# A fused attention and feed-forward kernel: the weight join, the casts and the order of the opening are changed

## The chip, the cores and the metric

The kernel runs on one NeuronCore of one Trainium2 chip. The metric is the device time of one execution in microseconds (us). The core has five engines that run side by side, each in the order of its own instruction queue: TensorE (PE in the profile, with PEld for its weight loads), VectorE (DVE), ScalarE (ACT), GpSimd (POOL) and SyncE (SP), which here only issues DMA transfers.

## The reference

Block-window attention with summaries, then a feed-forward layer with a piecewise gate. Only what matters:

```python
batch, n_heads, seq, head_dim = (4, 8, 768, 64)       # q, k, v, fp32
block, window = (32, 16)
k_sum = k.reshape(B, H, nb, block, D).max(axis=3)     # 24 summary keys per sequence
v_sum = v.reshape(B, H, nb, block, D).mean(axis=3)    # 24 summary values
scores = concat(window scores with |i - j| < 16, scores on k_sum + log(32))
x = softmax(scores) @ concat(v, v_sum)                # heads side by side: 3072 tokens x 512
h = x @ w_in                                          # 512 -> 2048
g = where(h >= 1, h, where(h <= -1, 0, (h + 1)**2 / 4))
out = g @ w_out                                       # 2048 -> 512
```

The weights w_in and w_out come as 64-bit floating-point numbers, which the engines don't compute with. So the kernel turns each into a 32-bit number from its two 32-bit words: sign, exponent and upper mantissa bits from the top word, the last three bits from the low word.

## The kernel before, in words

The 3072 tokens are worked through in eight chunks of 384 tokens (T), two for each sequence. A chunk's attention is done for four pairs of heads; its feed-forward (FF) layer runs over sixteen slices f of 128 hidden units. Products of the FF layer keep fp32 accuracy by splitting both operands into a high part (cast to fp32r) and the rest: three products for one.

The order is written out by hand. `OPENING`, `SECOND` and `LATER` are lists of steps; a step is a letter, which names a function in the table `steps`, and hexadecimal digits, its arguments. Each engine gets its instructions in the order of the list. `OPENING` covers all of chunk 0, the conversion of all weights and chunk 1's attention. `SECOND` and `LATER` run the FF layer of a chunk with the attention of the next between it; a step that was done already is skipped there.

The attention steps, by chunk, pair of heads and often head: `r`, `y` load the raw keys and values of a sequence for the summaries, `k`, `v`, `q` the windows and queries, `m` the mask and an identity matrix. `K` lays out chunk 0's key windows, `R` takes the summary keys (maximum), `C` copies them behind the windows, `Y`, `Z`, `V`, `W` do the same for the values: sum on VectorE, transpose on TensorE, mean on ScalarE (L267), spread over the six blocks on GpSimd (L271). `S` is the score product, `M` adds the mask and takes the maxima, `E` the exponentials, `D` the reciprocals (an add, L306, and a reciprocal, L307), `N` the norm on GpSimd (L311), `T` a transpose on TensorE, `P` its copy out, `A` the value product, `X` and `L` the high part and the rest of x.

The weight steps, for each of sixteen pairs of weight pieces (512 columns each): `w` fetches, `a` (L139) and `b` (L144) scale the top and the low word on ScalarE, `c` joins the words on VectorE, `d` casts to the high part (`convert_high`, on GpSimd for even pairs and ScalarE for odd ones), `e` subtracts it on GpSimd (L172). Pair i holds w_out's slice i-1 and w_in's slice i+1.

The FF steps: `F` (L421, four parts per slice) is the first product, `G`, `H`, `I`, `J` the gate and its high part, `O` (L450, GpSimd) the rest, `B` (L459) the second product. `U` and `o` take out and store the result.

`j` (L429) writes filler products on TensorE: fp32 products of a 128 x 128 tile of zeros with itself whose result nobody reads. The last digit of the step is their number.

Buffers limit how early a step can run: the tiles of kind "k", "q" and "v" have two buffers each; the converted words and the raw keys and values share three (`stage`, tag "w"); PSUM gives six banks to the joins and the attention of the opening, three of which hold the result of chunk 0 from its first `B` on.

Of the kernel before, what the change touches and what calls it, by code (L numbers as in the profile page):

```python
# [45 lines left out]
H01 G02 I01 H02 F030 F031 F032 I02 F033 F040 F041 w6 w7 w8 a6 w9 F042 F043 J01 b6 b7 c5 O01 G03 H03 I03 B01 d4 e4
F050 F051 d5 F052 F053 J02 J03 O02 B02 O03 B03 v10 v11 a7 a8 a9 e5 G04 G05 H04 H05 b8 c6 c7 d6 d7 e6 e7 I05 F060 F061
F062 F063 q10 q11 I04 F070 F071 F072 F073 J04 O04 J05 O05 B04 B05 b9 c8 c9 d8 e8 wa aa ba wb ab bb G06 H06 I06 J06
F080 F081 F082 F083 O06 B06 ca d9 e9 da ea G07 H07 I07 F090 F091 G08 H08 I08 F0a0 F0a1 F0a2 F0a3 F092 F093 J07 J08
# [533 lines left out]
```

## Time and profile before

| | us |
|---|---|
| median of 3 runs | 657.27 |
| lowest and highest | 656.46, 657.53 |
| profiled execution, its time | 656.5 |
| profiled execution, its span | 654.5 |
| TensorE busy | 630.8 (96%) |
| VectorE busy | 372.3 (57%) |
| ScalarE busy | 345.1 (53%) |
| GpSimd busy | 259.4 (40%) |

The span is the time from the first to the last instruction in the trace; the 2.0 us between it and the execution's time lie around it. Busy time of TensorE counts the filler products too. A row of a profile names the source line (L421), the engine, the operation, what is written and read, the number of instructions, and in brackets what ended the idle time in front of them.

### The profile page before, as it was taken

What the parts mean: (1) busy time and instruction counts of PE and PEld (TensorE: products, weight loads), DVE (VectorE), ACT (ScalarE), POOL (GpSimd) and SP (SyncE); (2) the same over time, 40 slices, a digit from 0 to 9 for tenths busy, and PEclk for the clock granted to TensorE, in tenths of its full rate; (3) what the DMA queues carried; (4) which work ended last, traced back from release to release, by engine and by line L of the source; (5) the groups of instructions that cost most, each with busy time, mean ns of one, the idle gap of its engine ahead of it and who ended that gap; (6) DMA issues with size and microseconds to landing.
All of it is one profiled execution on the core that took longest, in us unless ns stands there. A gap on an engine that the chain in (4) does not pass through costs nothing.

```text
span 654.5 us, 11884 instructions
## 1 busy us (share of the span) xinstructions
PE 630.8 (96%) x4442; PEld 561.3 (86%) x4442; DVE 372.3 (57%) x837; ACT 345.1 (53%) x881; POOL 259.4 (40%) x272
## 2 busy tenths in 40 slices
PE   7789999679999999999999999999999999999997
PEld 7688997568898989889898988889898888999996
DVE  5899983638773735838571746838671744511111
ACT  3789974735454645454454645444364636433332
POOL 1659985524342333333333333324333332322221
PEclk9989999889999999999999999999999999999999
DMA  8999700474121325034301324034211410000001
GB/s 283 326 343 296 268 2 22 134 227 142 40 69 38 117 61 143 28 89 135 88 21 37 119 61 143 18 89 144 74 35 37 118 37 2 2 21 29 1 1 48
DMA packets 49769, 63.57 MB, mean 97 GB/s; under 512 B 24880, under 2 KB 33328, under 8 KB 49712
## 3 DMA queue, kind: packets, MB, share of 16 engines
q1 hardware_dynamic: 49712, 62.81, 31.4%
q8 instruction: 35, 0.57, 0.4%
q14 instruction: 22, 0.18, 0.1%
HBM read 56.51 MB, written 6.29 MB: 96 GB/s over the span
## 4 chain that ended last, share of the span: by engine, by line
PE 85%; DVE 4%; DMA 4%; POOL 2%; ACT 2%; issue 2%; SPq 1%; POOLq 0%; ACTq 0%; DVEq 0%
PE acc L459 39%; PE h L421 37%; PE o_ps L410 3%; DMA first<-in_kT 3%; PE s_ps L355 2%; PE o_ps L327 1%; DMA vraw<-in_vT 1%; PE t_ps L316 1%; POOL glo L450 1%; DVE turned_blocks L400 1%; ACT e L301 1%; POOL halves L172 1%; PE h_idle L429 1%; DVE w L159 0%; PE s_ps L283 0%
## 5 line engine op out<-in xcount | busy, mean ns | idle before, releaser
L421 PE MATMUL h<-xhi,halves 128*128 128x384 f32 x1024 | 283.9, 339 | 2.2 <-DVE t L440 1.6
L459 PE MATMUL acc<-halves,ghi 128*128 128x512 f32 x768 | 240.7, 394 | 0.0
L450 POOL TENSOR_TENSOR glo<-t,ghi 128x384 fp32r<-128x384 f32 x128 | 130.0, 1017 | 267.4 <-ACT ghi L445 173.8
L421 PEld LDWEIGHTS h<-xhi,halves 128*128 128x128 f32 x1024 | 188.0, 188 | 9.0 <-issue 2.2
L440 DVE SCALAR_TENSOR_TENSOR t<-h,t 128x384 f32<-128x384 f32 x128 | 71.2, 557 | 215.1 <-ACT t L437 204.7
L421 PE MATMUL h<-xlo,halves 128*128 128x384 f32 x512 | 173.5, 339 | 0.0
L459 PEld LDWEIGHTS acc<-halves,ghi 128*128 128x128 f32 x768 | 144.8, 188 | 28.7
L459 PE MATMUL acc<-halves,glo 128*128 128x512 f32 x384 | 154.6, 402 | 0.4 <-POOL glo L450 0.4
L434 ACT ACTIVATE t<-h,ones_half 128x384 f32<-128x384 f32 x128 | 74.2, 580 | 123.2 <-PE h L421 119.8
L445 ACT CAST ghi<-t 128x384 fp32r<-128x384 f32 x128 | 65.4, 513 | 119.8 <-DVE t L440 119.4
L400 DVE STREAM_TRANSPOSE turned_blocks<-e 32x192 f32<-32x192 f32 x288 | 106.5, 370 | 22.0 <-POOL e L388 17.9
L421 PEld LDWEIGHTS h<-xlo,halves 128*128 128x128 f32 x512 | 96.5, 188 | 5.4
L459 PEld LDWEIGHTS acc<-halves,glo 128*128 128x128 f32 x384 | 72.1, 188 | 15.1 <-issue 1.9
L437 ACT ACTIVATE t<-t 128x384 f32<-128x384 f32 x128 | 66.9, 523 | 3.2
L376 ACT ACTIVATE e<-e,den 128x120 f32<-128x120 f32 x144 | 55.3, 387 | 24.2 <-DVE den L370 24.2
L388 POOL TENSOR_TENSOR e<-e,den 128x720 f32<-128x720 f32 x24 | 33.4, 1391 | 48.7 <-DVE den L382 25.5
L172 POOL TENSOR_TENSOR halves<-w,halves 128x1024 fp32r<-128x1024 f32 x16 | 38.6, 2416 | 3.3 <-ACT halves L166 2.7
L376 ACT ACTIVATION_READ_ACCUMULATOR e<-e,den 128x1 f32 x144 | 27.5, 191 | 0.0
L429 PE MATMUL h_idle<-zeros 128*128 128x128 f32 x162 | 23.4, 304 | 1.0 <-POOL zeros L112 1.0
L301 ACT ACTIVATE e<-e,den 128x120 f32<-128x120 f32 x48 | 18.3, 384 | 10.7 <-DVE den L296 10.6
L429 PEld LDWEIGHTS h_idle<-zeros 128*128 128x128 f32 x162 | 21.8, 216 | 1.6 <-POOL zeros L112 1.0
L363 DVE SCALAR_TENSOR_TENSOR e<-s_ps,mask_sb 128x360 f32<-128x360 f32 x48 | 22.2, 524 | 0.0
(78 smaller groups left out, 455.0 us busy)
## 6 DMA issues: line engine op xcount, KB each, us to landing
k<-in_kwin SPq DMA_DIRECT2D x28, 360.0 KB, 4.1
v<-in_vwin SPq DMA_DIRECT2D x30, 288.0 KB, 3.3
raw<-in_w_in SPq DMA_DIRECT2D x16, 512.0 KB, 10.4
raw<-in_w_out SPq DMA_DIRECT2D x16, 512.0 KB, 10.6
out<-o SPq DMA_DIRECT2D x24, 256.0 KB, 2.3
q<-in_q SPq DMA_DIRECT2D x56, 96.0 KB, 4.2
kraw<-in_kT SPq DMA_DIRECT2D x13, 384.0 KB, 4.6
vraw<-in_vT SPq DMA_DIRECT2D x13, 384.0 KB, 5.8
```

The source lines that it names most:

```text
L172: nc.gpsimd.tensor_tensor(out=lo, in0=converting[i].bitcast(F32), in1=hi.bitcast(F32), op=ALU.subtract)
L376: nc.scalar.activation(out=e, in_=e, func=AF.Exp, bias=dens[c, p][:, 0, j, t:t + 1], scale=1.0, accum_out=dens[c, p][:, 1, j, t:t + 1])
L388: nc.gpsimd.tensor_tensor(out=e, in0=e, in1=den.unsqueeze(2).broadcast_to([P, 2 * NT, KA]), op=ALU.mult)
L400: nc.vector.transpose(out=pt[kb * SB:(kb + 1) * SB, :, qb * SB:(qb + 1) * SB], in_=e[qb * SB:(qb + 1) * SB, :, at:at + SB])
L421: nc.tensor.matmul(hs[c, f][:, :T], weight["win", f][w][:, k * P:(k + 1) * P], x, start=(k == 0 and n == 0), stop=(k == NK - 1 and n == 2))
L429: nc.tensor.matmul(hs["idle"][:, :P], zeros, zeros, start=True, stop=True)
L434: nc.scalar.activation(out=ts[c, f], in_=hs[c, f][:, :T], func=AF.Relu, bias=ones_half, scale=0.5)
L437: nc.scalar.square(out=ts[c, f], in_=ts[c, f])
L440: nc.vector.scalar_tensor_tensor(out=ts[c, f], in0=hs[c, f][:, :T], scalar=1.0, in1=ts[c, f], op0=ALU.max, op1=ALU.min)
L445: nc.scalar.copy(out=hi, in_=ts[c, f])
L450: nc.gpsimd.tensor_tensor(out=lo, in0=ts[c, f], in1=hi.bitcast(F32), op=ALU.subtract)
L459: nc.tensor.matmul(acc[c][i], a[:, rows], weight["wout", f][w], start=(f == 0 and n == 0), stop=(f == NF - 1 and n == 2))
```

## The change

- The join (`c`) is done in two instructions for each half of a pair instead of three. The first shifts the top word left by three and ORs the low word into it; the second ORs the sign bit in. The integer add is gone. Since the low word is now ORed, `b` scales it so that it never exceeds seven. The four instructions of a pair are four steps of their own in the list (`c10` to `c13`).
- All casts to the high part (`d`) run on GpSimd. The subtractions (`e`) of pairs 1, 5, 9 and 13 run on VectorE, the others stay on GpSimd.
- The value means are kept in a tile of their own for each pair of heads, so that chunk 1, of the same sequence, only spreads them again (`W`): its steps `Z` and `V` are gone, and `W` writes six blocks where it wrote five.
- `M` is cut into a mask step `M` and a maximum step `f` for each head, `m` into mask and identity.
- `OPENING` has a new order. Chunk 1's attention stands between the FF steps of chunk 0, further first products of chunk 1 and loads for chunk 2 stand in it, and its `j` steps are others.

```diff
@@ the order of the opening, up to chunk 0's first FF product and a little beyond
 OPENING = """
-m r00 K00 R00 C00 q00 r01 R01 q01 K01 C01 y01 j00f S00 j013 S01 M00 M01 E000 D000 E001 D001 y00 E010 N000 j02e T000
-P000 E011 r02 K02 R02 C02 q02 Y01 N001 j038 T001 w0 a0 D010 N010 Y00 j041 Z00 Z01 r03 K03 v00 v01 V00 W00 D011 N011
-R03 C03 P001 y02 S02 M02 b0 c0 d0 e0 E020 V01 W01 j054 A00 T010 P010 T011 P011 q03 j063 S03 M03 X00 L00 E021 D021
-N021 D020 N020 Y02 j07f j085 Z02 w1 a1 E030 D030 N030 y03 E031 D031 N031 Y03 j096 Z03 b1 c1 w2 b2 a2 v02 V02 W02 A01
-X01 T021 P021 T020 P020 L01 c2 w3 b3 a3 v03 V03 W03 j0a4 A02 T031 P031 T030 P030 j0b3 A03 X02 L02 d1 d2 X03 L03 w4 a4
-b4 c3 F000 F001 F002 F003 G00 H00 I00 F010 F011 F012 F013 e1 F020 c4 F021 F022 F023 e2 w5 a5 b5 J00 O00 B00 d3 e3 G01
...
+q00 r00 r02 R00 K00 C00 r01 m0 q02 j00f j01f j02f j03f S00 R02 M000 K01 f000 R01 q01 K02 w0 M001 r03 C01 E000 D000 C02
+j04f j059 S01 M010 f010 E010 y02 f001 y01 N000 y00 M011 f011 m1 j065 S02 E001 b0 D001 a0 N001 v00 j07f j08f j099 T000
+K03 R03 T001 P001 P000 Y00 Z00 w1 c01 M020 C03 c00 V00 W00 M021 E011 q03 v01 y03 D010 f021 N010 D011 E021 Y01 f020
+j0af j0b2 A00 c03 c02 N011 j0cf j0d2 S03 Y02 b1 T010 T011 E020 M030 M031 d0 X00 Z01 V01 D021 a1 Z02 W01 P010 V02 P011
+w2 j0ef j0f2 A01 N021 f030 E030 D020 Y03 T021 L00 N020 T020 f031 X01 E031 v02 e0 D030 L01 v03 F000 Z03 c10 F010 W02
+P021 c12 c11 P020 b2 a2 N030 F001 c13 V03 A02 D031 X02 T030 c20 P030 c21 N031 L02 T031 w4 k10 q10 F011 w3 q11 P031 W03
+d1 k11 A03 X03 c23 F002 a4 w6 c22 d2 L03 F003 e1 F012 F013 G00 H00 G01 C10 H01 I00 I01 S10 M101 e2 f101 w7 b4 c40 J00
+c41 J01 F020 c42 F021 F022 F030 O01 F031 b3 w5 F032 F023 O00 c43 d4 F033 M100 a3 C11 k12 G02 B00 f100 c31 q12 c30 c32
...
-HI_POOL = [0, 2, 4, 6, 8, 10, 12, 14]
+REST_VECTOR = [1, 5, 9, 13]
...
-        nc.scalar.mul(out=low, in_=low.bitcast(U32), mul=2.0 ** -29)
-
-    def convert_join(i):
+        nc.scalar.mul(out=low, in_=low.bitcast(U32), mul=7.49 * 2.0 ** -32)
+
+    def convert_join(i, n):
 
         low, top = raws[i]
-        w = converting[i] = stage.tile([P, 2 * DM], I32, tag="w", name=f"w{i}", bufs=W_BUFS)
-        c_ps = [ps.tile([P, DM], I32, tag="ps", name=f"c{i}_{part}") for part in range(2)]
-        cols = [slice(part * DM, (part + 1) * DM) for part in range(2)]
-        for part in range(2):
-            nc.vector.tensor_scalar(out=c_ps[part], in0=top[:, cols[part]], scalar1=3, scalar2=0x7FFFFFF8,
-                                    op0=ALU.logical_shift_left, op1=ALU.bitwise_and)
-        for part in range(2):
-            nc.vector.scalar_tensor_tensor(out=c_ps[part], in0=top[:, cols[part]], scalar=-0x80000000, in1=c_ps[part],
+        what, part = divmod(n, 2)
+        cols = slice(part * DM, (part + 1) * DM)
+        if what == 0:
+            joined[i, part] = ps.tile([P, DM], I32, tag="ps", name=f"c{i}_{part}")
+            nc.vector.scalar_tensor_tensor(out=joined[i, part], in0=top[:, cols], scalar=3, in1=low[:, cols],
+                                           op0=ALU.logical_shift_left, op1=ALU.bitwise_or)
+        else:
+            if i not in converting:
+                converting[i] = stage.tile([P, 2 * DM], I32, tag="w", name=f"w{i}", bufs=W_BUFS)
+            nc.vector.scalar_tensor_tensor(out=converting[i][:, cols], in0=top[:, cols], scalar=-0x80000000, in1=joined[i, part],
                                            op0=ALU.bitwise_and, op1=ALU.bitwise_or)
-        for part in range(2):
-            nc.vector.tensor_tensor(out=w[:, cols[part]], in0=c_ps[part], in1=low[:, cols[part]], op=ALU.add)
 
     def convert_high(i):
         halves[i] = room(i, "halves", [P, 2, 2 * DM], F32R)
-        if i in HI_POOL:
-            nc.gpsimd.tensor_copy(out=halves[i][:, 0], in_=converting[i].bitcast(F32))
-        else:
-            nc.scalar.copy(out=halves[i][:, 0], in_=converting[i].bitcast(F32))
+        nc.gpsimd.tensor_copy(out=halves[i][:, 0], in_=converting[i].bitcast(F32))
...
     def convert_rest(i):
         hi, lo = halves[i][:, 0], halves[i][:, 1]
-        nc.gpsimd.tensor_tensor(out=lo, in0=converting[i].bitcast(F32), in1=hi.bitcast(F32), op=ALU.subtract)
+        eng = nc.vector if i in REST_VECTOR else nc.gpsimd
+        eng.tensor_tensor(out=lo, in0=converting[i].bitcast(F32), in1=hi.bitcast(F32), op=ALU.subtract)
...
-        nc.scalar.mul(out=v_ts[c, p][KW:KA, 0], in_=vs_pss[c, p][:NSUM, :P], mul=1.0 / SB)
+        v_mean[p] = att.tile([P, P], F32, tag=f"mean{p}", name=f"mean{c}_{p}", bufs=1)
+        nc.scalar.mul(out=v_mean[p][KW:KA], in_=vs_pss[c, p][:NSUM, :P], mul=1.0 / SB)
 
     def spread_vals(c, p):
-        mean = v_ts[c, p][KW:KA]
-        nc.gpsimd.tensor_copy(out=mean[:, 1:], in_=mean[:, :1].broadcast_to([NSUM, NB - 1, P]))
+        nc.gpsimd.tensor_copy(out=v_ts[c, p][KW:KA], in_=v_mean[p][KW:KA].unsqueeze(1).broadcast_to([NSUM, NB, P]))
...
-    def masks(c, p):
+    def masks(c, p, j):
...
+    def maxima_of_head(c, p, j):
...
-        if "idle" not in hs:
-            hs["idle"] = ps_h.tile([P, 512], F32, tag="h", name="h_idle")
+        if ("idle", stage_) not in hs:
+            hs["idle", stage_] = ps_h.tile([P, 512], F32, tag="h", name=f"h_idle{stage_}")
         for _ in range(n):
-            nc.tensor.matmul(hs["idle"][:, :P], zeros, zeros, start=True, stop=True)
+            nc.tensor.matmul(hs["idle", stage_][:, :P], zeros, zeros, start=True, stop=True)
```

More of the change, by code (lines that the diff above doesn't have):

```diff
@@ L45 @@
-b4 c3 F000 F001 F002 F003 G00 H00 I00 F010 F011 F012 F013 e1 F020 c4 F021 F022 F023 e2 w5 a5 b5 J00 O00 B00 d3 e3 G01
[L46 to L49, printed above, removed]
@@ L50 @@
-O07 B07 O08 B08 wc ac wd we bc bd be cb db eb cc G09 H09 I09 F0b0 F0b1 G0a H0a I0a F0c0 F0c1 J09 J0a F0c2 F0b2 F0b3
-F0c3 ad cd ae O09 G0b H0b B09 I0b O0a B0a G0c H0c I0c dc dd ec ed F0d0 F0d1 F0d2 F0e0 F0e1 F0e2 F0e3 F0d3 J0b O0b J0c
-B0b O0c B0c k10 C10 k11 C11 ce de ee wf af bf cf df ef G0d H0d I0d F0f0 F0f1 F0f2 J0d F0f3 G0e H0e I0e J0e O0d B0d
-O0e G0f H0f I0f J0f O0f B0e B0f U02 o02 S10 k12 U01 o01 q12 U00 o00 S11 q13 k13 Z10 V10 W10 Z11 V11 Z12 W11 M10 E100
-Z13 E101 M11 E110 D100 N100 T100 D101 N101 T101 C12 D110 N110 C13 E111 D111 N111 P100 P101 S12 M12 A10 v12 X10 L10
@@ L57 @@
+H0e I0e D131 cf3 N131 A12 G0f X12 B0c H0f N130 q20 J0e T130 T131 P131 I0f L12 F110 F100 F111 P130 W13 A13 J0f F101 df
+F102 O0e ef X13 L13 k21 F112 F103 B0d G10 O0f F113 G11 H11 I11 B0e H10 I10 B0f F120 F121 J11 O11 J10 O10 F122 F123 U02
+o02 U01 U00 o00 o01
 """
@@ L116, in fused_kernel @@
     pairs = [pieces[2 * i:2 * i + 2] for i in range(NF)]
-    weight, raws, converting, halves = {}, {}, {}, {}
+    weight, raws, converting, joined, halves = {}, {}, {}, {}, {}
     def room(i, what, shape, dtype):
@@ L285, in scores @@
         s_pss[c, p] = s_ps
[L287 removed]
+    def masks(c, p, j):
         at = c % NHALF
[L289 to L296 removed]
+        es[c, p, j] = att.tile([P, NT, KA], F32, tag=f"e{j}", name=f"e{c}_{p}_{j}", bufs=E_BUFS)
+        nc.vector.scalar_tensor_tensor(
+            out=es[c, p, j], in0=s_pss[c, p][j][:, :NT * KA].rearrange("p (t n) -> p t n", n=KA), scalar=1.0 / math.sqrt(D),
+            in1=mask_sb[:, at:at + NT], op0=ALU.mult, op1=ALU.add)
+    def maxima_of_head(c, p, j):
+        dens[c, p, j] = att.tile([P, 2, NT], F32, tag=f"den{j}", name=f"den{c}_{p}_{j}")
+        nc.vector.tensor_reduce(out=dens[c, p, j][:, 0], in_=es[c, p, j], axis=AX.X, op=ALU.max, negate=True)
     def exps(c, p, j):
@@ L471, in store, with load_constants @@
         nc.sync.dma_start(out=out[c * T + i * P:c * T + (i + 1) * P, :], in_=outs[c, i])
-    def load_constants():
-        for i in range(2):
-            rows = slice(i * QB, (i + 1) * QB)
-            nc.sync.dma_start(out=mask_sb[rows], in_=mask[rows, i:i + NT + 1])
-        nc.sync.dma_start(out=ident_sb, in_=ident)
+    def load_constants(n):
+        if n == 0:
+            for i in range(2):
+                rows = slice(i * QB, (i + 1) * QB)
+                nc.sync.dma_start(out=mask_sb[rows], in_=mask[rows, i:i + NT + 1])
+        else:
+            nc.sync.dma_start(out=ident_sb, in_=ident)
     steps = {
         "m": load_constants, "r": load_raw_keys, "k": load_keys, "q": load_queries, "y": load_raw_vals, "v": load_vals, "w": fetch,
-        "K": window_keys, "R": sum_keys, "C": summary_keys, "S": scores, "M": masks, "E": exps, "D": reciprocals, "N": norms,
+        "K": window_keys, "R": sum_keys, "C": summary_keys, "S": scores, "M": masks, "f": maxima_of_head, "E": exps, "D": reciprocals, "N": norms,
         "T": transposes, "P": turned, "Y": sum_vals, "Z": turn_vals, "V": mean_vals, "W": spread_vals, "A": values, "X": high,
```

24 lines of the change are left out of this document (12 added, 12 removed).

## The prediction

> **What bounds the kernel now.** I read the page's first part and then its time by stretches, because an average over 654 us hides where TensorE (PE) stands still.
>
> ```profile
> span 654.5 us, 11884 instructions
> PE 630.8 (96%) x4442; PEld 561.3 (86%) x4442; DVE 372.3 (57%) x837; ACT 345.1 (53%) x881; POOL 259.4 (40%) x272
> ```
>
> Five stretches follow: up to chunk 0's first feed-forward (FF) product, chunk 0's FF, chunk 1's attention with the start of its FF, the later chunks, the end. Columns: length, then busy time of PE, PEld, DVE, ACT, POOL with instructions, granted clock, DMA share, GB/s.
>
> ```profile
> 0.00:42.25 42.25, 34.66 (x382) 31.17 (x383) 32.38 (x70) 25.62 (x73) 16.13 (x32) 0.96 0.98 309
> 42.25:111.70 69.45, 68.06 (x342) 60.57 (x338) 56.20 (x97) 55.96 (x81) 59.26 (x40) 1.00 0.54 170
> 111.70:163.30 51.60, 41.41 (x389) 34.82 (x389) 32.41 (x81) 29.46 (x107) 21.63 (x30) 0.90 0.57 166
> 163.30:600.00 436.70, 436.70 (x3091) 390.32 (x3092) 244.47 (x580) 214.87 (x586) 150.15 (x159) 1.00 0.23 67
> 600.00:654.50 54.50, 49.94 (x247) 44.42 (x245) 6.83 (x12) 19.23 (x36) 12.19 (x12) 1.00 0.04 15
> ```
>
> From 163 us PE never stops, and the change doesn't touch that part. What can move lies in the first three rows: 7.6, 1.4 and 10.2 us without a product, and clocks of 0.96 and 0.90 (34.66 x 0.04 = 1.4 us and 41.41 x 0.10 = 4.1 us). While the weights are joined (second row) PE is busy 68.06 of 69.45 us. The join, 56.20 us of VectorE (DVE) with the gates, is covered there; GpSimd (POOL) is the fullest helper, 59.26 of 69.45.
>
> The filler products matter most. The timeline of PE gives their price: each row is start, length and records.
>
> ```profile
> 0.99 6.10 PE L429 MATMUL h_idle<-zeros 128*128 128x128 f32 x30 [0.99 <-POOL zeros L112]
> 7.89 0.85 PE L283 MATMUL s_ps<-k,first 64*64 64x120 f32 x24 [0.81 <-POOL k L239]
> 25.92 4.73 PE L429 MATMUL h_idle<-zeros 128*128 128x128 f32 x40
> 42.25 0.44 PE L421 MATMUL h<-xhi,halves 128*128 128x384 f32 x1
> L429 PE MATMUL h_idle<-zeros x162: 272/275/582, 1.0 to 40.4; 128*128 128x128 f32 x162
> ```
>
> The old list asks for 81 filler products (the last digits of its `j` steps added up) and the trace has 162 records: a product is two records. The first 15 take 6.10 us. Later 40 records last 4.73 us; without the last one's own 0.275 us that is 4.455/39 = 0.114 us a record, 0.228 a product. They wait for nothing, so PE can't skip them.
>
> **The change part by part.** *Filler.* The new list has 179 products before F000: 60 before S00, then 24, 5, 39, and three times 17. The 98 more cost 98 x 0.228 = 22.3 us of PE. With 60 of them ahead, S00 can't start before 0.99 + 6.10 + 45 x 0.228 = 17.4 us; it now starts at 7.89. (At 0.114 a product it would be 7.8. The list reads as if a product were one record, but the rows say two.) The other pieces of PE work, from the chain of waits:
>
> ```profile
> 28.73 0.46 DVE xlo L338
> ...
> 34.70 0.21 PE vs_ps L263
> ...
> 38.37 0.85 PE o_ps L327 x24
> 39.22 0.82 PE t_ps L316 x6
> ...
> 41.35 0.38 ACT xhi L333
> ...
> 43.65 1.20 DVE c L153 x2
> ...
> 50.18 2.09 PE acc L459 x9
> 52.27 4.22 PE h L421 x24
> ...
> 111.76 0.79 PE s_ps L283 x24
> ```
>
> PE's work up to the end of step A01 is 1.0 head + 43.5 filler (6.1 + 164 x 0.228) + four S (3.2) + four T (1.6) + three Z (0.6) + two A (1.7) = 51.6 us; with T021 and T020 F000 starts at 52.4, against 42.25. All that these steps wait for is issued 10 us and more ahead in the new list, so I count no wait in front of F000: the 6.6 us of today (7.6 less the head's 0.99) and the 1.4 us of clock go into the filler.
>
> *Attention of chunk 1* moves from behind chunk 0's FF into it. Its waits (10.2 us), the slow clock (4.1) and the 1.4 us of the second row go if PE always finds work; four transposes of value sums go with certainty (4 x 0.21 = 0.8), their ACT copies lie aside. The early loads of chunk 2 (k, q, r of two pairs) belong to the same 10.2 us. The floor of the span, with no wait after F000, is
>
> 654.5 + 22.3 - 6.6 - 1.4 - 0.8 - (10.2 + 4.1 + 1.4) = 652.3 us.
>
> To it comes W, all PE waits after F000. The sum decides on W.
>
> *Fetch order.* k12 needs k10's buffer, free after S10, which PE reaches near 59 us; w8 and the fetches behind it on SP wait too. They are first needed by F090 near 90 us, so 30 us cover it: nothing.
>
> *Helpers.* These are the groups, with mean ns.
>
> ```profile
> L450 POOL TENSOR_TENSOR glo<-t,ghi 128x384 fp32r<-128x384 f32 x42 | 42.6, 1019 | 58.1 <-ACT ghi L445 29.2 <-PE acc L459 15.8 <-PE o_ps L410 4.0
> L172 POOL TENSOR_TENSOR halves<-w,halves 128x1024 fp32r<-128x1024 f32 x16 | 38.6, 2416 | 3.3 <-ACT halves L166 2.7
> L311 POOL TENSOR_TENSOR e<-e,den 128x360 f32<-128x360 f32 x16 | 12.5, 789 | 9.8 <-DVE den L306 5.3 <-ACT e L301 3.3 <-DVE den L307 0.8
> L166 ACT CAST halves<-w 128x1024 fp32r<-128x1024 f32 x8 | 8.4, 1050 | 4.6 <-DVE w L159 4.4
> L239 POOL COPY k<-ks 128x144 f32<-128x144 f32 x16 | 4.8, 306 | 19.4 <-DMA k<-in_kwin 10.9 <-DVE ks L236 8.4
> L271 POOL COPY v<-v 24x640 f32<-24x640 f32 x6 | 4.2, 716 | 5.0 <-ACT v L267 4.7
> ```
>
> A pair's join falls from six instructions to four of 0.60 us each (1.20 for two): 16 x 1.2 = 19 us of DVE. Eight casts (8 x 1.05 = 8.4 us) go from ACT to POOL; four subtractions leave POOL (4 x 2.42 = 9.7) for DVE. A subtraction there isn't shown: from two 512-wide joins (1.2 us) to L172's 2.42; I take 1.2, the same width on the same engine. spread_vals writes 768 elements, not 640: 0.86 for 0.72 us. The new factor in convert_low and the split of masks and maxima cost nothing, the same instructions; their cover is ACT and DVE idle time in the second row (13 us each), without which each ACT multiply would cost its 1.1 us.
>
> *What the join reads.* Each old join instruction has one operand in PSUM. The new shift-with-OR reads both its words from SBUF, as do the four moved subtractions. No such DVE instruction is in this trace. What it shows is that some SBUF-to-SBUF instructions are held by POOL:
>
> ```profile
> 14.42 0.79 POOL L311 TENSOR_TENSOR e<-e,den 128x360 f32<-128x360 f32 x1 [3.56 <-DVE den L306]
> 14.57 0.70 DVE L230 COPY first<-first 128x80 f32<-128x80 f32 x1
> 28.22 2.37 POOL L172 TENSOR_TENSOR halves<-w,halves 128x1024 fp32r<-128x1024 f32 x1
> 29.11 1.50 DVE L306 TENSOR_SCALAR den<-den 128x3 f32<-128x3 f32 x1
> L306 DVE TENSOR_SCALAR den<-den x16: 141/304/1505, 13.9 to 128.3; 128x3 f32<-128x3 f32 x16
> L156 DVE SCALAR_TENSOR_TENSOR c<-raw,c x32: 683/690/697, 24.5 to 98.3; 128x512 int32<-128x512 int32 x32
> L231 DVE COPY first<-first x1: 336/336/336, 15.2 to 15.2; 128x384 f32<-128x384 f32 x1
> ```
>
> A three-element add takes 0.14 us alone and 1.50 when it starts inside a POOL subtraction; it ends at 30.61, 0.02 after the subtraction (30.59). The copy at 14.57 ends 0.06 after POOL's product. The join with one SBUF word never stretches (683 to 697 ns). The held copies are fast ones: 384 elements in 0.34 us, where a 512-wide join needs 0.60; they take about two words at a time. The shift-with-OR takes two words at a time too, from two tensors. So the bounds are: never held, as L156, or held to the end of the POOL instruction each time, as L306. I take held, since two words from SBUF at a time is what the held rows share.
>
> The Trainium skill, "SBUF — State Buffer", section "Who interferes with whom", says that a VectorE instruction with two SBUF inputs and a GpSimd instruction that reads SBUF exclude each other for the whole instruction, and speaks against this change. The trace agrees for copies and scalar adds and can't show the two-input case; by the page W would be the sum below, by L156's row the one of the first rival.
>
> If they exclude each other, POOL and those DVE instructions share one line of time. It opens when pair 1 is joined: A01 51.6 + 0.4 (X01) + 0.5 (L01) + four joins 2.4 = 54.9 us. From there POOL has 15 casts 15.7, 11 subtractions 26.6, 16 gate remainders 16.3, chunk 1's 8 norms 6.3, 4 key and 4 value spreads 1.2 + 3.4: 69.5 us. DVE adds 28 shift-with-OR 16.8, four subtractions 4.8, 8 scalar adds 1.3: 22.9. 54.9 + 92.4 = 147.3, and the last FF2 step B0f then ends 2.1 later, 149.4. PE's own work up to there is 1.0 + 43.5 + eight heads' S, T, A (8 x 2.46 = 19.7) + four Z 0.8 + FF 16 x 4.2 = 67.2 + eight early FF1 steps of chunk 1 at 0.53 = 4.2: 136.4. **W = 149.4 - 136.4 = 13.0.** Span 652.3 + 13.0 = 665.3; the profiled execution took 656.5 for its span of 654.5, so 667.3; the median of the runs is 657.27, 0.8 above that execution: **668 us**.
>
> **The rivals.** *Not held.* POOL then ends at 54.9 + 69.5 + 2.1 = 126.5, before PE's 136.4, and W is only friction: the 1.4 us that the second row has now, 1 to 2 at F020 (pair 1's subtraction stands on DVE behind L03), 1 to 2.6 at the first scores of chunk 2. W = 3 to 7, say 4.5: 659.6 us. For it: L156's 683 to 697. Against it: the held rows.
>
> *Held, and each time by a whole POOL instruction*, since a waiting POOL goes next: 58 POOL instructions in 69.5 us are 1.2 us each, 40 DVE instructions wait 48 us on top of DVE's own 60 or so from 52.7 (60 joins 36.0, four subtractions 4.8, else gates and chunk 1's attention): 161 us, W about 27, 682 us. Against it: DVE's other half (sign-OR, gates, maxima) runs beside POOL and fills part of it.
>
> *PE always has work* (the side of faster). The second and third rows together hold 88.6 us of DVE, 85.4 of ACT and 80.9 of POOL beside 109.5 of PE, and the change takes 14 us from DVE and 8 from ACT, so the new order could leave no wait: 652.3 + 2.8 = 655.1 us. It decides only if W stays under 0.9. Against it: the stretch with no attention in it already has 1.4. With it I count the case that a filler product costs half, against the 162 records.
>
> **How the numbers follow.** Held 0.53; held with whole waits 0.12; not held 0.20, a quarter of it within the band; PE always busy 0.15, two thirds of it faster. About 0.2% (1.3 us, 656.0 to 658.6) is what a measurement of this kernel can tell from no change. So faster 0.10, same 0.10, slower 0.53 + 0.12 + 0.15 = 0.80. The range goes from 657, below most of the unheld case, to 680, most of the way into whole waits; the likeliest case alone is 664 to 675.
>
> **What the changed profile would show.** Filler: 358 records, S00 at 17.4, F000 at 52.4 us. An earlier F000 breaks the first term. Held: the shift-with-OR's longest far above its shortest 0.6 us, ending with POOL's instructions, and POOL's subtractions past 2.44 us. All shift-with-OR within 20 ns of 0.69 breaks it. W: PE waits between 55 and 150 us behind POOL's remainders and subtractions, some 13 us, B0f's end near 149. B0f ending near 137 with PE full would make me wrong, and the kernel as fast as before or faster.

## The result, and the profile after

| | before | after |
|---|---|---|
| median, us | 657.05 | 687.31 |
| lowest and highest, us | 656.46, 657.53 | 684.44, 689.02 |
| profiled span, us | 654.5 | 687.0 |

The kernel became slower: the ratio of after to before is 1.0457, with a 95% interval of 1.0420 to 1.0493. The direction was forecast, the size was not: 668 us, at most 680. The page's first part, after:

```profile
span 687.0 us, 12217 instructions
PE 657.7 (96%) x4634; PEld 586.5 (85%) x4634; DVE 384.5 (56%) x809; ACT 336.4 (49%) x869; POOL 270.9 (39%) x276
```

TensorE is 96% busy as before, so the page alone doesn't show where 32 us of the span went. The time by stretches does. Columns as in the prediction; the cuts are the first FF product, 100 us, the copy of chunk 0's result, and the point from which TensorE never stops.

```profile
0.00:52.40 52.40, 51.15 (x523) 49.35 (x523) 23.82 (x51) 17.39 (x57) 13.92 (x27) 1.00 1.01 300
52.40:100.00 47.60, 39.79 (x278) 32.86 (x275) 44.37 (x61) 34.97 (x71) 36.52 (x28) 0.89 0.60 185
100.00:162.70 62.70, 55.16 (x359) 47.40 (x359) 46.13 (x65) 38.24 (x86) 47.52 (x37) 0.95 0.20 64
162.70:180.00 17.30, 9.16 (x75) 7.79 (x74) 6.82 (x13) 2.69 (x5) 3.40 (x7) 0.83 0.74 207
180.00:633.00 453.00, 453.00 (x3165) 405.22 (x3165) 256.50 (x611) 224.09 (x618) 157.91 (x169) 1.00 0.23 68
```

The first row is full, most of it filler. In the second VectorE (third busy number) is at 44.37 of 47.60 us, the fullest helper, where GpSimd had been. TensorE idles 7.8 us there and 7.5 in the third row, and its clock is 0.89 and 0.95. In the fourth it does 9.16 us of work in 17.30. From 180 to 633 us nothing is lost, and the last 54 us are much as before (TensorE busy 49.42 us; 49.94 of the last 54.5 before).

The timeline shows the points that the prediction named: S00, the first FF product and the copy of the finished result (B0f's end).

```profile
0.99 16.47 PE L431 MATMUL h_idle<-zeros 128*128 128x128 f32 x120 [0.99 <-POOL zeros L116]
17.39 0.84 PE L285 MATMUL s_ps<-k,first 64*64 64x120 f32 x24
52.58 0.45 PE L423 MATMUL h<-xhi,halves 128*128 128x384 f32 x1
162.74 0.58 ACT L469 COPY o<-acc 128x512 f32<-128x512 f32 x1 [1.17 <-PE acc L461]
```

The groups of the conversion follow, with mean ns, up to 175 us; L157 is the shift-with-OR, L162 the sign-OR, L167 the cast, L174 the subtraction.

```profile
L157 DVE SCALAR_TENSOR_TENSOR c<-raw 128x512 int32<-128x512 int32 x32 | 40.4, 1288 | 1.4 <-ACT raw L148 1.1 <-ACT pt L322 0.2
L162 DVE SCALAR_TENSOR_TENSOR w<-raw,c 128x512 int32<-128x512 int32 x32 | 20.9, 676 | 0.3
L174 POOL TENSOR_TENSOR halves<-w,halves 128x1024 fp32r<-128x1024 f32 x12 | 31.5, 2628 | 0.5
L174 DVE TENSOR_TENSOR halves<-w,halves 128x1024 fp32r<-128x1024 f32 x4 | 9.0, 2242 | 0.4 <-POOL halves L167 0.2
```

And shortest, median and longest of single lines; L308 is an add of three elements:

```profile
L157 DVE SCALAR_TENSOR_TENSOR c<-raw x32: 687/1085/2909, 30.2 to 144.2; 128x512 int32<-128x512 int32 x32
L308 DVE TENSOR_SCALAR den<-den x16: 153/514/2299, 21.2 to 148.2; 128x3 f32<-128x3 f32 x16
L174 POOL TENSOR_TENSOR halves<-w,halves x12: 2368/2410/3234, 50.2 to 153.1; 128x1024 fp32r<-128x1024 f32 x12
```

The sign-OR has one word in PSUM and takes 676 ns; the shift-with-OR, of the same width, has both words in SBUF and takes 1288 in the mean, from 687 to 2909. The GpSimd subtraction, 2437 at most before, now reaches 3234.

### The profile page after: what moved, and what is told of

The parts are those of the page before. It is cut to its first block, busy times and chain, and to the rows that moved or that the text cites. A ratio compares the mean times of both kernels' runs of the same rounds, so it can differ in the third digit from the quotient of the medians.

```text
span 687.0 us, 12217 instructions
## 1 busy us (share of the span) xinstructions
PE 657.7 (96%) x4634; PEld 586.5 (85%) x4634; DVE 384.5 (56%) x809; ACT 336.4 (49%) x869; POOL 270.9 (39%) x276
## 4 chain that ended last, share of the span: by engine, by line
PE 85%; DVE 5%; DMA 4%; issue 2%; SPq 1%; ACT 1%; POOL 1%; DVEq 0%; POOLq 0%
PE h L423 36%; PE acc L461 36%; PE h_idle L431 6%; PE o_ps L412 3%; PE s_ps L357 2%; DVE c L157 2%; DMA q<-in_q 1%; DMA raw<-in_w_out 1%; DMA vraw<-in_vT 1%; PE s_ps L285 1%; DVE w L162 1%; PE t_ps L318 1%; DVE den L308 1%; DMA k<-in_kwin 1%; PE o_ps L329 0%
## 5 line engine op out<-in xcount | busy, mean ns | idle before, releaser
L423 PE MATMUL h<-xhi,halves 128*128 128x384 f32 x1024 | 291.6, 345 | 15.8 <-DVE t L442 8.4
L452 POOL TENSOR_TENSOR glo<-t,ghi 128x384 fp32r<-128x384 f32 x128 | 133.4, 1043 | 278.9 <-ACT ghi L447 181.2
L423 PEld LDWEIGHTS h<-xhi,halves 128*128 128x128 f32 x1024 | 191.5, 192 | 24.4 <-DVE e L365 5.9
L442 DVE SCALAR_TENSOR_TENSOR t<-h,t 128x384 f32<-128x384 f32 x128 | 70.9, 555 | 216.4 <-ACT t L439 209.5
L423 PE MATMUL h<-xlo,halves 128*128 128x384 f32 x512 | 175.8, 343 | 0.0
L423 PEld LDWEIGHTS h<-xlo,halves 128*128 128x128 f32 x512 | 98.2, 192 | 5.6 <-DVE xlo L340 0.3
L461 PEld LDWEIGHTS acc<-halves,glo 128*128 128x128 f32 x384 | 72.5, 189 | 15.8 <-issue 2.1
L431 PE MATMUL h_idle<-zeros 128*128 128x128 f32 x358 | 44.4, 287 | 1.0 <-POOL zeros L116 1.0
L431 PEld LDWEIGHTS h_idle<-zeros 128*128 128x128 f32 x358 | 43.3, 203 | 1.6 <-POOL zeros L116 1.0
L157 DVE SCALAR_TENSOR_TENSOR c<-raw 128x512 int32<-128x512 int32 x32 | 40.4, 1288 | 1.4 <-ACT raw L148 1.1
L174 POOL TENSOR_TENSOR halves<-w,halves 128x1024 fp32r<-128x1024 f32 x12 | 31.5, 2628 | 0.5
L303 ACT ACTIVATE e<-e,den 128x120 f32<-128x120 f32 x48 | 18.3, 383 | 22.9 <-DVE den L298 22.9
```

The source lines that it names most:

```text
L157: nc.vector.scalar_tensor_tensor(out=joined[i, part], in0=top[:, cols], scalar=3, in1=low[:, cols], op0=ALU.logical_shift_left, op1=ALU.bi ...
L423: nc.tensor.matmul(hs[c, f][:, :T], weight["win", f][w][:, k * P:(k + 1) * P], x, start=(k == 0 and n == 0), stop=(k == NK - 1 and n == 2))
L431: nc.tensor.matmul(hs["idle", stage_][:, :P], zeros, zeros, start=True, stop=True)
L442: nc.vector.scalar_tensor_tensor(out=ts[c, f], in0=hs[c, f][:, :T], scalar=1.0, in1=ts[c, f], op0=ALU.max, op1=ALU.min)
L452: nc.gpsimd.tensor_tensor(out=lo, in0=ts[c, f], in1=hi.bitcast(F32), op=ALU.subtract)
L461: nc.tensor.matmul(acc[c][i], a[:, rows], weight["wout", f][w], start=(f == 0 and n == 0), stop=(f == NF - 1 and n == 2))
```

## The experiments

Each kernel starts from the kernel after or the kernel before and is shown by what differs. Times of one execution are marked (1); the others are medians. On the chips of the four groups the kernel before took 656.8, 656.2, 655.8 and 656.0 us. The kernel after ranges from 684.4 to 689.0 us in its four executions, and the profiled one is the longest; so a single execution set against its median of 687.3 is uncertain by 2 or 3 us, and the row of -3.9 is hardly clear of that. Where a trace of one kernel is set against a trace of another, spans are compared.

| kernel | base | us | against |
|---|---|---|---|
| half the filler | after | 669.0 (1) | after: -18.3 |
| low word in PSUM | after | 677.7 (1) | after: -9.6 |
| chunk 2's keys later | after | 683.4 (1) | after: -3.9 |
| these three | after | 659.5 | before: 1.0044 [1.0030, 1.0059] |
| new join alone | before | 665.7 | before: 1.0135 [1.0103, 1.0166] |
| join, casts and subtractions | before | 673.7 (1) | before: +17.5 |
| room for chunk 2's keys | after | 680.8 (1) | after: -6.5 |
| filler, PSUM and room | after | 654.8 | before: 0.9986 [0.9970, 1.0002] |
| the same, casts shared | after | 658.4 | before: 1.0041 [1.0026, 1.0055] |
| low word in PSUM | before | 662.3 | before: 1.0108 [1.0081, 1.0135] |
| both keys early | after | 658.2 | before: 1.0031 [1.0017, 1.0044] |
| a third of the filler | after | 658.6 | before: 1.0038 [1.0022, 1.0054] |

**Half the filler.** Every `j` step writes half its products, 83 in all, about as many as the kernel before has (81).

```diff
-        for _ in range(n):
+        for _ in range(n // 2):
             nc.tensor.matmul(hs["idle", stage_][:, :P], zeros, zeros, start=True, stop=True)
```

> The changed kernel with 83 filler products instead of 179 (each filler step does half its number); all else as changed. Theory 'filler': the 96 products less are 96 x 0.228 = 21.9 us less on TensorE ahead of the first FF product, of which up to 6 us come back as waits there, since the attention of chunk 0 now waits for its data. First score product near 10 us, first FF product 31 to 37 us, time 667 to 673 us. Rival 'filler stands in waits anyway': the opening is paced by GpSimd, VectorE and the transfers, and less than 5 us is won: above 682 us.

669.0 us. The timeline of TensorE:

```profile
34.32 0.44 PE L423 MATMUL h<-xhi,halves 128*128 128x384 f32 x1 [1.50 <-POOL halves L174]
```

The first FF product comes 18.3 us earlier (52.58 - 34.32); the span falls by 20.1 (687.0 - 666.9), the time by 18.3 against the median. By the price of 0.228 us the 96 products were worth 21.9; 3.6 of it come back ahead of this product, 1.50 of these as the wait in the row. All as the theory said. So more than half of the 30 us is filler.

**The low word in PSUM.** ScalarE writes the scaled low word, in two halves, into the PSUM tile in which the join works, directly ahead of the shift-with-OR, which then has one word in SBUF.

```diff
     def convert_low(i):
-        low, _ = raws[i]
-        nc.scalar.mul(out=low, in_=low.bitcast(U32), mul=7.49 * 2.0 ** -32)
+        pass
...
+            nc.scalar.mul(out=joined[i, part], in_=low[:, cols].bitcast(U32), mul=7.49 * 2.0 ** -32)
             nc.vector.scalar_tensor_tensor(out=joined[i, part], in0=top[:, cols], scalar=3,
-                                           in1=low[:, cols],
+                                           in1=joined[i, part],
```

> The changed kernel, but ScalarE writes the scaled low word of each half pair into the PSUM bank of the join, directly ahead of the first of the two join instructions, so that the shift-with-OR reads one word from SBUF and one from PSUM. Same number of VectorE instructions, same order; ScalarE does two multiplies of 512 for one of 1024. Theory 'exclusion' (a VectorE instruction that reads two words from SBUF and a GpSimd instruction wait for each other): the shift-with-OR falls from a mean of 1.29 us to 0.69, GpSimd's subtraction from 2.63 to about 2.45, the last FF2 step of chunk 0 ends 12 to 18 us earlier than at 162.7, time 669 to 676 us. Rival 'order' (the waits come from where the steps stand): the instruction gets shorter but the time stays above 683 us.

677.7 us. The shift-with-OR of this kernel, by its line (shortest, median, longest) and by its group (mean, and idle time in front):

```profile
L157 DVE SCALAR_TENSOR_TENSOR c<-raw,c x32: 681/693/697, 37.2 to 133.6; 128x512 int32<-128x512 int32 x32
```

```profile
L157 DVE SCALAR_TENSOR_TENSOR c<-raw,c 128x512 int32<-128x512 int32 x32 | 21.6, 692 | 15.9 <-ACT c L156 15.8
```

None of the 32 stretches any more. So the stretching comes from the second word in SBUF. Chunk 0's result is copied at 151.26, 11.5 us earlier than 162.74, and the span ends 11.4 us earlier (675.6); against the median it is 9.6. The 12 to 18 us expected, and the range of the time, are just missed. One price is in the row: VectorE now waits 15.8 us for ScalarE's two multiplies, which stand so close ahead of it, 8.3 of it behind the first FF product.

**Chunk 2's keys later.** `r20` and `r21`, which load raw keys into two of the three staging buffers, are taken out of the opening; the list behind it loads them.

```diff
-... af r21 cd0 ... I0c H0d r20 J0c ...
+... af cd0 ... I0c H0d J0c ...
```

> The changed kernel without the two early loads of chunk 2's raw keys in the opening; the next list loads them, as in the kernel before. Theory 'buffers': the two loads hold two of the three buffers that the results also need, so chunk 0's three results leave one by one (162.7 to 168.5 us) and the raw values come after them. Without the two loads the second result doesn't wait 4.5 us for the first one's store, and TensorE's 5.5 us wait behind it goes or shrinks below 2: time 679 to 682 us. Rival 'the values are late in any case': TensorE still waits over 4 us there, above 685 us.

683.4 us, a little short of the expected fall, and part of it isn't the edit's: the first FF product comes at 51.21 here for 52.58, and the first load that was moved stands at 131.17 in the kernel after. From the copy of the result (160.11) to the end of the span (681.5) it takes 521.4 us for 524.3, so the edit brings 2.9. TensorE's waits behind the opening, from the list of its waits in the first 190 us, first of the kernel after, then of this one (engine, tile, line, releaser: us in all, times, longest):

```profile
PE h L423 <- DVE e L365: 5.5, 1, 5.5
PE s_ps L357 <- POOL k L241: 2.7, 1, 2.7
```

```profile
PE s_ps L357 <- POOL k L241: 7.5, 1, 7.5
```

The wait behind VectorE's mask (`e`) is gone, and the wait for the keys (`k`) has grown from 2.7 to 7.5: loaded late, they are late. Both orders lose time at this place.

**The three together.** The three edits above in one kernel.

> The changed kernel with half the filler, the low word in PSUM and the two key loads later: the three edits together. If the three causes are separate they add up: 687 - 17 - 14 - 7 = 649, between 644 and 654 us, and it is faster than the kernel before. If exclusion only showed because filler had delayed the rest, the sum falls short: 655 to 668 us. If the order itself costs, above 668 us.

659.5 us, 0.4% over the kernel before. The range for causes that add up is missed; the time lies in the one for a sum that falls short. The single gains add up to 31.8 us; 27.9 came.

**The new join alone, in the old order,** from the kernel before: only the arithmetic of `c` and its factor.

```diff
-        nc.scalar.mul(out=low, in_=low.bitcast(U32), mul=2.0 ** -29)
+        nc.scalar.mul(out=low, in_=low.bitcast(U32), mul=7.49 * 2.0 ** -32)
...
-            nc.vector.tensor_scalar(out=c_ps[part], in0=top[:, cols[part]], scalar1=3, scalar2=0x7FFFFFF8,
-                                    op0=ALU.logical_shift_left, op1=ALU.bitwise_and)
+            nc.vector.scalar_tensor_tensor(out=c_ps[part], in0=top[:, cols[part]], scalar=3, in1=low[:, cols[part]],
+                                           op0=ALU.logical_shift_left, op1=ALU.bitwise_or)
...
-            nc.vector.scalar_tensor_tensor(out=c_ps[part], in0=top[:, cols[part]], scalar=-0x80000000, in1=c_ps[part],
+            nc.vector.scalar_tensor_tensor(out=w[:, cols[part]], in0=top[:, cols[part]], scalar=-0x80000000, in1=c_ps[part],
...
-            nc.vector.tensor_tensor(out=w[:, cols[part]], in0=c_ps[part], in1=low[:, cols[part]], op=ALU.add)
```

> The kernel before with the new join alone (shift-with-OR of two SBUF words, then sign-OR; factor of the low word as changed); order, casts, subtractions and filler as before. Theory 'exclusion': the shift-with-OR's mean is above 0.9 us with a longest above 2, GpSimd's subtractions get longer, and chunk 0's FF stretch, 69.5 us now with GpSimd busy 59.3 of it, grows to 75 or more: 662 to 670 us. Rival 'order': VectorE has 12 instructions' time to spare per ten pairs and the join got 1.2 us a pair shorter, so the time is that of before within 1 us, 656 to 658.

665.7 us, as the theory said: slower by 9.5 with a third of the join's instructions gone. Its groups:

```profile
L153 DVE SCALAR_TENSOR_TENSOR c<-raw 128x512 int32<-128x512 int32 x32 | 41.7, 1346 | 1.7 <-ACT raw L139 1.7
L170 POOL TENSOR_TENSOR halves<-w,halves 128x1024 fp32r<-128x1024 f32 x16 | 41.0, 2567 | 2.5 <-ACT halves L164 1.9
L162 POOL CAST halves<-w 128x1024 fp32r<-128x1024 f32 x8 | 10.2, 1273 | 2.5 <-ACT xhi L331 2.5
```

The kernel before, for the same work:

```profile
L159 DVE CUSTOM_DVE_ANT_0 w<-raw,c 128x1024 uint16<-128x1024 uint16 x32 | 20.5, 685 | 0.0
L153 DVE TENSOR_SCALAR c<-raw 128x512 int32<-128x512 int32 x32 | 20.5, 688 | 1.7 <-ACT raw L139 1.7
...
L164 POOL CAST halves<-w 128x1024 fp32r<-128x1024 f32 x8 | 8.4, 1045 | 4.4 <-ACT e L301 3.6 <-DMA raw<-in_w_in 0.8
```

One instruction of 1346 ns stands where these two, the shift and the integer add, stood, so VectorE saves next to nothing, and GpSimd's casts go from 1045 to 1273, its subtractions from 2416 to 2567.

**Join, casts and subtractions, in the old order**: the same with all casts on GpSimd and four subtractions on VectorE, as in the kernel after.

```diff
-HI_POOL = [0, 2, 4, 6, 8, 10, 12, 14]
+HI_POOL = list(range(16))
+REST_VECTOR = [1, 5, 9, 13]
```

> The kernel before with the new join, all casts on GpSimd and the subtractions of pairs 1, 5, 9, 13 on VectorE; order and filler as before. Theory 'exclusion': about as the join alone, 662 to 672 us, since GpSimd gains 8.4 us of casts and loses 9.7 us of subtractions; what is left to 687 us is then the order with its filler. Rival 'the arithmetic makes all of it': 683 us or more. Rival 'order makes all of it': 656 to 659 us.

673.7 us, 8.0 more than the join alone and a little over the range. The moved work costs in the old order too; casts and subtractions were moved in one edit, so their shares are not told apart. The VectorE subtraction takes 2171 ns in the mean.

**Room for chunk 2's keys.** The first raw key tile of chunk 2 gets a buffer of its own, the second is loaded into it as soon as the first is summed, and both sums and copies stand first in the list behind the opening; the results find all three staging buffers free. To make the room, the zeros lie in the opening's pool and the four mean tiles in one.

```diff
+        if what == "kraw" and (c, p) in ((2, 0), (2, 1)):
+            tag, bufs = "ahead", 1
...
-... af r21 cd0 ...
+... af cd0 ...
 SECOND = """
-v+0 v+1 F.00 ...
+R+0 C+0 r+1 R+1 C+1 v+0 v+1 F.00 ...
```

> The kernel after, with the wait behind the opening taken apart by room: the first of chunk 2's raw key tiles gets a buffer of its own, the second is loaded into it as the first step behind the opening, and both are summed there, so that all three staging buffers are free for the three results. Two small tiles are moved to make the room (the filler's zeros into the opening's pool, the four mean tiles into one). Theory (the two key tiles in the results' buffers are what makes 687.0 - 162.7 = 524.3 us behind the opening instead of 515.9): the copy of the result on VectorE no longer waits 4.53 us, chunk 2's masks no longer wait behind the value sums for their raw tile, and the time is 676 to 682 with the result copies still at 162 to 163. Rival (TensorE would wait for something else of chunk 2 in any case): 684 to 688, with the wait under another name.

680.8 us, in the theory's range. The result is copied at 160.87 here, 1.9 us earlier, which the theory had not in it. From there to the end of the span it takes 518.1 us (679.0 - 160.87), where the kernel after takes 524.3 and the prediction's sum 515.9: 6.2 of the 8.4 us are back. What is left stands mostly as one wait (TensorE's waits):

```profile
PE s_ps L360 <- POOL k L243: 4.2, 2, 3.8
```

**Filler, PSUM and room**: this kernel with the first two edits.

> The order of the kernel after with half the filler, the low word's multiply into PSUM in front of the join, and the room for chunk 2's keys of the run before this one (the run with the first three undone had the keys late instead). Theory (filler, exclusion and the buffers behind the opening are the three causes of the loss): 646 to 653, under the kernel before. Rival (something else of the new order costs as much): 655 to 660, as with the keys merely moved later (657.8).

654.8 us: the new order no longer loses, and is 0.14% under the kernel before with an interval that just includes no change. The theory's range is missed by 2 us, the rival's by 0.2. The three single gains (18.3, 9.6, 6.5) are 34.4 and would give 652.9.

**The same, casts shared**: the odd casts back on ScalarE, all subtractions back on GpSimd.

```diff
-REST_VECTOR = [1, 5, 9, 13]
+HI_SCALAR = [1, 3, 5, 7, 9, 11, 13, 15]
```

> The run before this one, with eight of the sixteen casts back on ScalarE and all subtractions back on GpSimd. Theory (the subtractions on VectorE, 2 us each with both engines held, still cost time): VectorE's small adds no longer wait up to 2.3 us, and the time falls by 1 to 5 us against the run before this one. Rival (ScalarE, which now also makes two multiplies of 0.64 us a block, sets the pace with the casts of about 1.1 us on top): slower by 1 to 6 us.

658.4 us, 3.6 slower: the theory fails, the rival holds. A wait of GpSimd between 20 and 140 us:

```profile
POOL halves L176 <- ACT halves L168: 11.4, 5, 4.8
```

The subtractions wait 11.4 us for ScalarE's casts, and VectorE's shift-with-OR waits 20.6 us for its multiplies there (10.2 in the run before, from 20 to 135 us). In this order with the low word in PSUM, the moved casts and subtractions are a gain.

**The low word in PSUM, in the old order**, from the kernel before (added lines; the sign-OR then writes `w`).

```diff
+            nc.scalar.mul(out=c_ps[part], in_=low[:, cols[part]].bitcast(U32), mul=7.49 * 2.0 ** -32)
+            nc.vector.scalar_tensor_tensor(out=c_ps[part], in0=top[:, cols[part]], scalar=3, in1=c_ps[part],
+                                           op0=ALU.logical_shift_left, op1=ALU.bitwise_or)
...
```

> The kernel before, with the two-instruction join whose low word lies in PSUM (ScalarE's multiply writes the two halves there directly ahead of the join); casts, subtractions, order and filler as before. Theory (the two words in SBUF are the whole harm of the new join, and VectorE's two passes fewer in a block are worth something): 646 to 656, no POOL subtraction over 2.5 us. Rival (VectorE isn't what the opening waits for, and the multiplies so late make it wait for ScalarE): 656 to 662. The same join with two words in SBUF took 665.7.

662.3 us: only 3 us better than with two words in SBUF, and just over the rival's range. The stretching is gone (the shift-with-OR takes 685 to 697 ns, no GpSimd subtraction over 2427), but VectorE now waits for ScalarE's late multiplies; that this wait makes all of the 6 us over the kernel before is not shown. VectorE's longest wait in the first 120 us:

```profile
DVE c L154 <- ACT c L152: 18.5, 9, 6.8
```

**Both keys early; a third of the filler.** First the second keys are loaded early too, into a staging buffer; then, on top of it, the filler is cut from a half to a third.

```diff
-        if what == "kraw" and (c, p) in ((2, 0), (2, 1)):
+        if what == "kraw" and (c, p) == (2, 0):
...
-R+0 C+0 r+1 R+1 C+1 v+0 v+1 F.00 ...
+R+0 C+0 R+1 C+1 v+0 v+1 F.00 ...
...
-        for _ in range(n // 2):
+        for _ in range(n // 3):
```

> The kernel of the run with half the filler, the low word in PSUM and a buffer of its own for chunk 2's first keys (654.8 us), with the second keys loaded early too, into a staging buffer, so that the third result waits for their sum instead of TensorE for their load. Theory (the 3.85 us that TensorE's scores waited for GpSimd's k behind the opening were the late second load): 650.5 to 653.5, about 3 us less. Rival (the third result's copy on ScalarE, which now waits, delays the gate behind it): 654 to 656.

> The run before this one with a third of the kernel after's filler (each step's count divided by 3 and rounded down) instead of half. Theory (in this order filler stands in front of work that has its data ready): some 26 products fewer at 0.228 us are up to 6 us, and the time is 645 to 650. Rival (with half of it TensorE waits already, and what is taken out comes back as waits for VectorE, GpSimd and loads ahead of the first FF1 product): within 1 us of the run before.

658.2 and 658.6 us: neither gains. The first loses about 3 and is above both of its ranges; the second, 0.4 us from the first, is as its rival said. The first's timeline, a row of VectorE and one of TensorE, behind the opening:

```profile
144.36 0.95 DVE L253 TENSOR_REDUCE sums<-vraw 128x24 f32<-128x768 f32 x1 [7.49 <-DMA vraw<-in_vT]
147.43 0.69 PE L426 MATMUL h<-xhi,halves 128*128 128x384 f32 x1 [5.92 <-DVE e L368]
```

With the keys in time, TensorE reaches the FF product sooner and waits there for the masks, which stand behind the value sums in VectorE's queue, and these wait 7.49 us for their raw values. Early keys move the stall from the keys to the values. In the second kernel the first FF product comes at 35.31 us, with the filler of the first at 35.27: what was taken out came back as waits. The transposes wait, for one, for their identity matrix, which had hidden behind filler (1.3 us before, 2.9 now).

At a half, then, TensorE already runs at the speed of its loads and helpers up to its first FF product.

## Why the prediction was wrong, step by step

**Filler: right.** 358 records, S00 at 17.39 for 17.4, the first FF product at 52.58 for 52.4, hardly a wait ahead of it but the head's (51.15 of 52.40 us busy). Halving it brought the first FF product 18.3 us forward, between the 22.3 of product time and the 15.7 that remain of it with the 6.6 of waits that I had it absorb. (The 7.8 for S00 at 0.114 us a product leaves out the slow first records: 0.99 + 6.10 + 30 x 0.114 is 10.5. Nothing hangs on it.)

**Fetch order at nothing: right.** The loads that stood behind k12 went out late, but neither scaling of the weights on ScalarE waited for one: no idle time stands ahead of either from 52.4 to 163 us. The low word's group:

```profile
L148 ACT ACTIVATE raw<-raw 128x1024 int32<-128x1024 uint32 x14 | 16.1, 1148 | 0.0
```

**Held or not: right.** The shift-with-OR's longest is four times its shortest, and GpSimd's subtractions pass 2.44 us. GpSimd and VectorE in the timeline, twice, with the TensorE wait that ends at the second place:

```profile
82.34 2.73 POOL L174 TENSOR_TENSOR halves<-w,halves 128x1024 fp32r<-128x1024 f32 x1
81.52 4.10 DVE L157 SCALAR_TENSOR_TENSOR c<-raw 128x512 int32<-128x512 int32 x2
113.50 3.19 POOL L174 TENSOR_TENSOR halves<-w,halves 128x1024 fp32r<-128x1024 f32 x1
112.45 2.05 DVE L174 TENSOR_TENSOR halves<-w,halves 128x1024 fp32r<-128x1024 f32 x1
114.42 2.30 DVE L308 TENSOR_SCALAR den<-den 128x3 f32<-128x3 f32 x1
116.85 0.53 DVE L442 SCALAR_TENSOR_TENSOR t<-h,t 128x384 f32<-128x384 f32 x1
117.43 0.69 PE L423 MATMUL h<-xhi,halves 128*128 128x384 f32 x1 [4.33 <-DVE t L442]
```

In the second place the VectorE subtraction ends at 114.50 and GpSimd's, whose row starts inside it, at 116.69, 2.19 later, where one takes 2.4 alone. The add of three elements then lasts until 116.72. Each stands in the other's way, and TensorE's longest wait, 4.33 us, is for the gate step (L442) that stands behind the two in VectorE's queue. The shift-with-OR and the subtraction are the case of two SBUF inputs of the Trainium skill, "SBUF — State Buffer", section "Who interferes with whom", which the trace of before could not show; with one word in PSUM (681 to 697 ns) the shift-with-OR isn't held, as that section also says.

**W = 13.0: the step that failed.** B0f ended near 162.7, not 149.4, so W was 26.3 where the sum had 13.0. TensorE's idle time in the second and third row is 7.8 + 7.5 = 15.3 us and the slow clock takes 39.79 x 0.11 + 55.16 x 0.05 = 7.1. Some 4 us are TensorE's own work, priced too low: it was busy 51.15 + 39.79 + 55.16 = 146.1 us up to there, 139.0 without the clock's part, where the sum had 135.4 and the head. What it waited for in the two rows, the longest:

```profile
PE h L423 <- DVE t L442: 8.4, 4, 4.3
PE t_ps L318 <- POOL e L313: 2.3, 2, 1.9
PE t_ps L318 <- DVE w L162: 2.0, 1, 2.0
PE h L423 <- POOL halves L174: 1.5, 2, 0.9
```

The prediction expected some 13 us of waits behind GpSimd's remainders and subtractions. Those are 2.0 us (1.5 for the subtractions, 0.5 for the remainders); 11.0 of the 15.3 were waits for VectorE, 8.4 of them for its gate step. So the path was another than the one that the sum followed. Two things were missing in it. First, it put all of GpSimd's work and the held VectorE instructions on one line of time, each at its length alone, and let the rest of VectorE's work pass beside it for nothing. But a VectorE that is held does none of the rest either, and from 52.4 to 100 us it was the fullest helper. From 52.4 to 163 us:

```profile
L157 DVE SCALAR_TENSOR_TENSOR c<-raw 128x512 int32<-128x512 int32 x30 | 39.0, 1327 | 1.1 <-ACT raw L148 1.1
L308 DVE TENSOR_SCALAR den<-den 128x3 f32<-128x3 f32 x10 | 6.5, 648 | 0.0
L452 POOL TENSOR_TENSOR glo<-t,ghi 128x384 fp32r<-128x384 f32 x18 | 21.5, 1206 | 9.4 <-ACT ghi L447 6.9 <-PE acc L461 2.4
```

30 x (1327 - 692) = 19.1 us and 10 x (648 - 153) = 5.0 us are VectorE standing in its own instructions, with 153 ns the shortest of L308 (such adds were held before the change too: all sixteen took 7.0 us before and 9.4 after); the four subtractions add 4 x (2242 - 1200) = 4.2 over what I took for them. In kind that is the rival of whole waits, which I gave 0.12 and which put the end of this work at 161 us and the time at 682. In size it isn't: a held shift-with-OR waited 0.64 us (1327 - 692), not 1.2, and the 48 us of waiting were 28. That 161 comes so near to 162.7 is luck in part.

The kernel with the low word in PSUM shows how much of W hangs on the second SBUF word: B0f comes 11.5 us earlier. W is still 14.9 there (151.26 - 136.4), more than the 3 to 7 of the rival without a hold. The four subtractions and the small adds are still held in it, and VectorE waits for ScalarE; how the 14.9 divide was not tested.

Second, I took the clock as full from the first FF product on; it was 0.89 and 0.95. Read in stretches of 0.2 us, the granted clock of the kernel after is 1.00 or 0.50 but for the edges. Between 52.4 and 162.7 us it is at 0.50 in three spells, 58.0 to 61.6, 88.8 to 95.8 and 116.0 to 123.0, and each begins inside a TensorE wait or within 0.3 us behind it: waits of 1.89, 1.97 and 4.33 us, while one of 1.49 us is followed by none. With the low word in PSUM the waits at these places are 1.25, 1.41 and 2.93 us, and only the last has a spell, 108.2 to 111.8. So the low clock went with the longer waits; what length it takes is not shown.

**"The early loads of chunk 2 belong to the same 10.2 us": wrong.** I let the stall behind the opening vanish in the new order. The prediction had not looked at the buffers these loads take. The timeline of the kernel after, SP's queue, VectorE, ScalarE:

```profile
163.35 5.17 SPq L473 DMA_DIRECT2D out<-o  x3
...
169.60 0.88 SPq L219 DMA_DIRECT2D vraw<-in_vT  x2
165.50 0.69 DVE L467 COPY o<-acc 128x512 f32<-128x512 f32 x1 [4.53 <-DMA out<-o]
175.23 0.95 DVE L251 TENSOR_REDUCE sums<-vraw 128x24 f32<-128x768 f32 x1 [7.32 <-DMA vraw<-in_vT]
167.08 0.58 ACT L469 COPY o<-acc 128x512 f32<-128x512 f32 x1 [3.76 <-DVE ks L238]
```

Two of the three staging buffers hold chunk 2's keys. VectorE's copy of the second result waits 4.53 us until the first is stored, the third waits for the key sum that stands behind that copy, SP stores over 5.17 us and only then loads the raw values, and the masks stand behind the value sums; TensorE waits 5.49 us for them, up to 178.35. From B0f to the end it took 524.3 us where the floor left 515.9: 8.4 us too much, of which the run with room for the keys took back 6.2. 13.3 + 8.4 = 21.7 us is the whole distance between the forecast span, 665.3, and 687.0.

**Where the 30 us lie.** Against the median the filler has 18.3, the second SBUF word 9.6 and the keys' buffers 6.5, each remedied alone; with all three remedied, the rest of the change (order, casts, means) is level with the kernel before, 0.9986. With the keys loaded later, as in the kernel before, in place of a buffer of their own it is 1.0044. The single gains exceed the joint one by 1.9 us against the median and by 6.7 in spans (20.1 + 11.4 + 8.0 for 32.8), so how far the three overlap is not settled. What remains open is why the new order, with 83 products of filler and most of the lock gone, gains nothing. Its clock between the first FF product and the result's copy is still 0.95, and VectorE waits 10.2 us for ScalarE's multiplies from 20 to 135 us (time by stretches of that kernel).

```profile
34.30:135.20 100.90, 91.77 (x632) 78.53 (x633) 73.19 (x126) 74.12 (x167) 75.94 (x64) 0.95 0.57 170
```

A part of the lock is left in it too. TensorE's longest wait in that stretch, 3.18 us up to 92.55, is again for a gate step on VectorE behind a subtraction (1.53 us) and an add of three elements (2.30) that ran beside a GpSimd subtraction of 3.19.

## What to carry to other kernels

When an edit puts two engines on one lock, the waits have to be added to the engine that waits, with all that is queued behind it; a sum of the locked work alone is too small. Filler written into a fixed order is work like any other, and its price is read from its records. A load that is moved ahead takes its buffer along: see who needs that buffer between the load and its use, because here the loads were in time and the results were not.

## What was not expected of the hardware

- The lock costs both sides. With the second word in SBUF the shift-with-OR took 1288 ns for 692, GpSimd's gate remainders 1206 for 1019 (kernel after, from 52.4 to 163 us, and kernel before), its casts 1273 for 1045 (the join alone in the old order, and kernel before).
- An instruction of three elements lasted 2.30 us behind a GpSimd subtraction, fifteen times its shortest, 0.15.
- A VectorE subtraction of 1024 elements with both words in SBUF took the 1.2 us of the prediction only as its shortest, in three kernels (1209 to 1216 ns), and 2.02 at the least in the kernel after. Its mean was 2242 ns in the kernel after, 1857 with the low word in PSUM and 2171 with join, casts and subtractions in the old order, whose row this is:

```profile
L172 DVE TENSOR_TENSOR halves<-w,halves x4: 1209/2030/3417, 47.8 to 104.0; 128x1024 fp32r<-128x1024 f32 x4
```

- ScalarE's two multiplies into PSUM cost little more than the one into SBUF: 2 x 629 = 1258 ns for two times 512 elements (kernel before with the low word in PSUM), 1148 for 1024 in the kernel after.

```profile
L152 ACT ACTIVATE c<-raw 128x512 int32<-128x512 uint32 x32 | 19.0, 629 | 1.7 <-DVE w L157 1.7
```
